# A gated mix of linear attention and an MLP: three of the four row blocks form the MLP's first layer from seven products of half tiles instead of eight

## The chip, the core and the metric

The kernel runs on one core of one Trainium2 chip. The metric is the device time of one execution in microseconds (us), as the median of several runs.

## The reference

```python
x = A_x                                        # 2048 x 512
g = sigmoid((x * gate_w).sum(-1, keepdims=True))
qkv = x @ wqkv                                 # 32 heads of width 16
pq, pk = q @ w_phi, k @ w_phi                  # per head
phi = concat(softmax(p), softmax(-p))          # for pq and for pk
kv, z = phi_k^T v, sum of phi_k                # per head, over all rows
a = (phi_q kv / (phi_q z + 1e-6)) @ wo
b = mish(x @ w1 + b1) @ w2                     # 512 -> 1376 -> 512
out = g * a + (1 - g) * b
```

## The kernel before

**Two passes.** The first pass (`a_ops`, line 289) goes over the 2048 rows in eight chunks of 256: it forms k, v and q, the features of k, the sums `kv` and `z`, and parks q in DRAM (`pqd`). Beside it `w_ops` (line 367) loads the MLP's weights in pieces and splits them. The second pass (`b_ops`, line 512) goes over four blocks of 512 rows, called block 0 to 3 here: it forms phi_q, the attention's output, the MLP and the mix, and stores the result.

**Precision.** Every operand of a large product is a pair of tiles, a rounded high part (`fp32r`) and the rest. A product of two such operands is three matmuls: high by high, high by low, low by high.

**The MLP in a block.** The hidden layer has 11 tiles of 128 units (`ORDER`, line 32); the first one, tile 5, is short and carries the gate's row too. For tile number i of a block: `up` (line 516) is 12 matmuls of 128x128 weights by 128x512 rows of x; `mi` is Mish with the bias on ScalarE (ACT); `hi` rounds to the high part on ACT; `lo` is the low part on GpSimd (POOL); `dn` (`down`, line 559) multiplies by the second layer into four PSUM tiles, 12 matmuls. `df` is `down` of the last tile, `fi` (line 712) mixes and stores one of the four row tiles.

**The attention in a block**, for row tile t: `lq` loads q (SP queue), `mx mn d0 d1` on VectorE (DVE) subtract the extremes, `E` is Exp on ACT, `S T rS D m de rd sc es` on DVE are sums, the denominator and the scaling, `tr` transposes on DVE and stores to DRAM (`ed`); `mv` (line 643) loads two of them back as `eT` with eight DMAs, `nu` multiplies by `kv`, `oh` (ACT) and `ol` (DVE) split the result, `wo` (line 676) is the last product, `ag` (ACT) applies the gate. `gr` takes the gate's row through DRAM and back, `ge gg` make the gate of it. `LX` loads the next block's x, `XH` (ACT) and `XL` (DVE) split it (`x_ops`, line 416).

**What sets the order.** Each engine works through its own queue in the order in which the program issues, and an instruction that waits holds up all behind it; SP's queue of DMA issues is such a queue too. The order is written out by hand in the step tables (lines 37 to 86): `run` (line 201) goes through a table and calls the steps; a step with `+` belongs to the next block, with `'` to the one before. Nothing is moved afterwards (`keep_in_program_order`).

**Buffers.** A tag has a fixed number of buffers which its tiles take in turn, so that a tile waits for the last use of an older one: tag `a` has 3 PSUM tiles (`up`, part of `nu`, every second `wo`), `dn` 4, `kv` 1; `oh` has 2 SBUF tiles (raw weights, the split `nu`), `tx` 2 (raw x, the products `T`), `pq` 3, `eT` 2.

Line 101 of the profile is the helper for every matmul, line 121 that for every ACT instruction.

Of the kernel before, what the change touches and what calls it, by code (L numbers as in the profile page):

```python
# [30 lines left out]
GROW = FA % P  # L31
ORDER = [NFA - 1] + list(range(NFA - 1)) + list(range(NFA, NF))
WARM = 10

# [37 lines left out]
    up0 mi0 hi0 lo0 gr mx2 mn2 d02 d12 mx3 mn3 d03 d13 up1 mi1 hi1 lo1 lq0+ lq1+ E2 E3 hc S2 T2 rS2 D2 m2 de2 rd2 sc2 es2 tr2  # L72
    up2 mi2 hi2 lo2 dn0 S3 T3 rS3 D3 m3 de3 rd3 sc3 es3 tr3 mv1 up3 mi3 hi3 lo3 dn1 up4 mi4 hi4 lo4 dn2
    mx0+ mn0+ d00+ d10+ mx1+ mn1+ d01+ d11+ lq2+ lq3+ up5 mi5 hi5 lo5 dn3 E0+ E1+ ge gg
    S0+ T0+ rS0+ D0+ m0+ de0+ rd0+ sc0+ es0+ tr0+ up6 mi6 hi6 lo6 dn4 up7 mi7 hi7 lo7 dn5 cd nu0 nu1 oh0 ol0 S1+ T1+ rS1+ D1+ LX0 LX1
    m1+ de1+ rd1+ sc1+ es1+ dn6 wo0 ag0 wo1 ag1 oh1 ol1 tr1+ mv0+ dn7 up8 mi8 hi8 lo8 mx2+ mn2+ d02+ d12+ mx3+ mn3+ d03+ d13+
    wo2 ag2 up9 mi9 hi9 lo9 dn8 E2+ E3+ up10 mi10 hi10 lo10 wo3 ag3 XH0+ XL0+ XH1+ XL1+ dn9 df0 fi0 df1 fi1 df2 fi2 df3 fi3
"""
BLOCK = """
    up0 mi0 hi0 lo0 gr lq0+ lq1+ S2 T2 rS2 D2 m2 de2 rd2 sc2 es2 tr2 up1 mi1 hi1 lo1 hc up2 mi2 hi2 lo2 dn0  # L80
    S3 T3 rS3 D3 m3 de3 rd3 sc3 es3 tr3 mv1 up3 mi3 hi3 lo3 dn1 up4 mi4 hi4 lo4 dn2
    mx0+ mn0+ d00+ d10+ mx1+ mn1+ d01+ d11+ lq2+ lq3+ up5 mi5 hi5 lo5 dn3 E0+ E1+ ge gg
    S0+ T0+ rS0+ D0+ m0+ de0+ rd0+ sc0+ up6 mi6 hi6 lo6 dn4 cd nu0 nu1 oh0 ol0 es0+ tr0+ S1+ T1+ rS1+ D1+ LX0 LX1 m1+ de1+ rd1+ sc1+
    es1+ dn5 wo0 ag0 wo1 ag1 oh1 ol1 tr1+ mv0+ dn6 up7 mi7 hi7 lo7 wo2 ag2 mx2+ mn2+ d02+ d12+ mx3+ mn3+ d03+ d13+
    up8 mi8 hi8 lo8 dn7 E2+ E3+ up9 mi9 hi9 lo9 wo3 ag3 up10 mi10 hi10 lo10 dn8 XH0+ XL0+ XH1+ XL1+ dn9 df0 fi0 df1 fi1 df2 fi2 df3 fi3
"""
# [3 lines left out]
def tile_gated_mix(ctx: ExitStack, tc: tile.TileContext, xT, wv, wkT, wqT, bd, w1a, w1b, b1, w2a, w2b, wo, out):  # L90
# [303 lines left out]

# [19 lines left out]
    wob = {}  # L414

    def x_ops(b, load, split):

        raw = {}
        for h in range(2):
            def ld(h=h):  # L420
                raw[h] = k4("xraw", "tx")
                pin(Sy.dma_start(kt(raw[h], SC), xT[2 * b + h]))
# [89 lines left out]
    def b_ops(b):  # L512
        key = ("B", b)
        U, dn, eTs, num, ohl, io, ed = {}, {}, {}, {}, {}, {}, {}

        def up(i):
            f = ORDER[i]
            xh, xl = xb[b]
            ps = psum("up", "a")
            n = 0  # L520
            for w, a in ((0, xh), (1, xh), (0, xl)):
                for k in range(KT):
                    mm(ps, w1_tile(f, w, k), a[:, k, :], start=(n == 0), stop=(n == 3 * KT - 1))
# [35 lines left out]
        def down(i, t):  # L559
            if t not in dn:  # L560
                dn[t] = psum("down", "dn")
            f = ORDER[i]
            h, l = [U[i][x][:, t * P : (t + 1) * P] for x in "hl"]
            for n, (a, w) in enumerate(((h, w2_tile(f, 0)), (h, w2_tile(f, 1)), (l, w2_tile(f, 0))) if i else ((h, w2x["a"]), (l, w2x["b"]))):
                mm(dn[t], a, w, start=(i == 0 and n == 0), stop=(i == (NF - 3 if t == last_t else NF - 1) and n == 2))

# [325 lines left out]
```

## Time and profile before

| | us |
|---|---|
| median of 3 runs (lowest, highest) | 444.73 (444.40, 446.12) |
| span of the profiled execution | 442.5 |
| first pass, to the first `up` | 149.4 |
| block 0, block 1, block 2 (first `up` to first `up`) | 72.5, 72.3, 72.4 |
| block 3 to the end of the span | 76.0 |
| busy in the span: TensorE (PE), DVE, ACT, POOL | 437.8, 313.2, 201.4, 159.6 |

The time of the profiled execution itself is not listed apart from its span; the span runs from its first to its last instruction, and the median of the runs is 2.2 us above it. In the views that follow, "L101 PE MATMUL" names the line of the kernel, the engine and the operation; `out<-in` are tiles by their names in the program. In a list by time, the first column is the start and the second the length, both in us; several equal instructions in a row are merged (`x12`). What stands in brackets at the end of a row is the idle time ahead of it and what ended it. SPq is SP's queue of DMA issues; its rows are the issues, not the transfers.

### The profile page before, as it was taken

The page shows a single profiled execution, that of the slowest core. Times are in us where ns is not written, and L with a number is a line of the kernel's source. Part 1 is how long each engine was busy: PE and PEld are TensorE (multiplying, and loading weights), DVE is VectorE, ACT ScalarE, POOL GpSimd, SP SyncE. Part 2 cuts the span into 40 slices and gives each one's busy share as a digit, 9 for nine tenths or more (in the row PEclk, how much of TensorE's full clock was granted, in tenths as well). Part 3 has the DMA queues.
Part 4 walks back from the last instruction along what each step waited for, and adds up shares of the span by engine and source line. Part 5 has one row for each costly group of instructions (what it writes and reads, how often), then busy time and mean ns, then how long its engine had stood idle before and what let it go on. Part 6 is the DMA issues. An engine that isn't in the chain of part 4 may idle for free.

```text
span 442.5 us, 7179 instructions
## 1 busy us (share of the span) xinstructions
PE 437.8 (99%) x2874; PEld 359.9 (81%) x2874; DVE 313.2 (71%) x420; ACT 201.4 (46%) x286; POOL 159.6 (36%) x100
## 2 busy tenths in 40 slices
PE   8999999999999999999999999999999999999996
PEld 7888888888888888887888878888878888887885
DVE  3987739559699999999999898279679329601103
ACT  3644523533345455736376533646352645341330
POOL 3078694785662453621024120215310222411121
PEclk9999999999999999999999999999999999999999
DMA  7721631524403136425362533222605302310002
GB/s 265 283 96 48 191 120 50 188 86 133 167 29 116 49 84 209 142 101 168 128 205 96 159 124 120 75 96 95 191 0 192 94 2 96 134 57 1 0 0 96
DMA packets 29001, 49.64 MB, mean 112 GB/s; under 512 B 6308, under 2 KB 15012, under 8 KB 28968
## 3 DMA queue, kind: packets, MB, share of 16 engines
q1 hardware_dynamic: 28648, 48.79, 32.9%
q8 instruction: 22, 0.36, 0.3%
q10 hardware_dynamic: 288, 0.39, 0.3%
q14 instruction: 11, 0.09, 0.1%
q0 software_dynamic: 32, 0.01, 0.0%
HBM read 31.73 MB, written 16.79 MB: 110 GB/s over the span
## 4 chain that ended last, share of the span: by engine, by line
PE 98%; DMA 1%; SPq 0%; DVE 0%; issue 0%
PE proj L101 30%; PE up L101 27%; PE down L101 27%; PE wo L101 10%; PE kvp L101 2%; PE num L101 2%; DMA wT<-in_wkT_dram 1%; PE fuse L101 1%; PE rest L101 0%; DVE io L709 0%; SPq L157 0%; SPq L149 0%
## 5 line engine op out<-in xcount | busy, mean ns | idle before, releaser
L543 POOL TENSOR_TENSOR l<-act,h 128x512 fp32r<-128x512 f32 (+1 forms) x44 | 62.6, 1425 | 215.5 <-ACT h L121 192.7
L121 ACT ACTIVATE act<-up,b1s 128x512 f32<-128x512 f32 x44 | 30.3, 688 | 83.1 <-PE up L101 81.0
L330 POOL TENSOR_TENSOR zacc<-zacc,E 128x1024 f32<-128x1024 f32 x16 | 39.7, 2479 | 39.9 <-DVE E L287 31.4
L121 ACT ACTIVATE E<-E 128x1024 f32<-128x1024 f32 x32 | 33.5, 1060 | 36.0 <-DVE E L272 35.9
L287 DVE TENSOR_TENSOR E<-E,Sm 128x1024 f32<-128x1024 f32 x32 | 45.1, 1409 | 1.0
L101 PE MATMUL wo<-woh,ohl 128*128 128x512 f32 x128 | 41.2, 389 | 0.0
L276 DVE TENSOR_REDUCE Sm<-E 128x64 f32<-128x1024 f32 x32 | 38.5, 1204 | 0.0
L101 PE MATMUL down<-w2ah,h 128*128 128x512 f32 x96 | 37.6, 392 | 0.0
L101 PE MATMUL down<-w2al,h 128*128 128x512 f32 x80 | 31.2, 390 | 0.0
L101 PE MATMUL down<-w2ah,l 128*128 128x512 f32 x80 | 31.1, 389 | 0.0
L121 ACT ACTIVATE h<-act 128x512 fp32r<-128x512 f32 (+2 forms) x48 | 30.3, 632 | 1.6
L101 PE MATMUL down<-w2bh,h 128*128 128x512 f32 x78 | 30.6, 392 | 0.0
L101 PE MATMUL down<-w2bl,h 128*128 128x512 f32 x78 | 30.4, 389 | 0.0
L101 PE MATMUL down<-w2bh,l 128*128 128x512 f32 x78 | 30.4, 389 | 0.0
L431 DVE TENSOR_TENSOR xbl<-xraw,xbh 128x1024 fp32r<-128x1024 f32 x8 | 10.9, 1378 | 27.1 <-ACT xbh L121 27.1
L256 DVE TENSOR_REDUCE mx<-proj 128x32 f32<-128x512 f32 x16 | 11.0, 689 | 25.5 <-PE proj L101 25.5
L101 PEld LDWEIGHTS wo<-woh,ohl 128*128 128x128 f32 x128 | 24.0, 188 | 5.0
L121 ACT ACTIVATE io<-wo,g_sb 128x512 f32<-128x512 f32 x16 | 11.0, 690 | 36.0 <-PE wo L101 34.7
L121 ACT ACT_TABLE_LOAD x19 | 24.4, 1283 | 3.5 <-PE up L101 3.2
L101 PE MATMUL up<-xbh,w1ah 128*128 128x512 f32 x96 | 25.8, 390 | 0.0
L101 PE MATMUL up<-xbh,w1al 128*128 128x512 f32 x96 | 25.7, 389 | 0.0
L101 PE MATMUL up<-xbl,w1ah 128*128 128x512 f32 x96 | 25.7, 389 | 0.0
(125 smaller groups left out, 978.3 us busy)
## 6 DMA issues: line engine op xcount, KB each, us to landing
ed<-E SPq DMA_DIRECT2D x16, 512.0 KB, 2.9
eT<-ed SPq DMA_DIRECT2D x64, 128.0 KB, 3.2
xraw<-in_xT_dram SPq DMA_DIRECT2D x15, 512.0 KB, 4.3
pqd<-qs SPq DMA_DIRECT2D x16, 256.0 KB, 2.1
pq<-pqd SPq DMA_DIRECT2D x16, 256.0 KB, 3.8
out_dram<-io SPq DMA_DIRECT2D x15, 256.0 KB, 2.0
raw<-in_w1a_dram SPq DMA_DIRECT2D x3, 512.0 KB, 4.6
raw<-in_w2a_dram SPq DMA_DIRECT2D x3, 512.0 KB, 3.7
```

Of the source, the lines that this page charges most:

```text
L101: return pin(nc.tensor.matmul(*a, **k))
L121: return pin(A_.activation(out_, in_, fn, **k))
L256: pin(V.tensor_reduce(d[name], hv(src()), axis=AX.X, op=op))
L276: pin(V.tensor_reduce(d["S"], hv(d["E"][:, :]), axis=AX.X, op=ALU.add))
L287: pin(eng.tensor_mul(hv(d["E"][:, :]), hv(d["E"][:, :]), d["S"][:, :, None].to_broadcast([P, 2 * H, DH])))
L330: at(key, f"z{t}", lambda d=d: pin(G_.tensor_add(zacc, zacc, d["E"])))
L431: pin(V.tensor_sub(xb[b][1][:, :, sl], kt(raw[h], SC), f32(xb[b][0][:, :, sl])))
L543: pin(G_.tensor_sub(U[i]["l"][:n, :], U[i]["a"][:n, :], f32(U[i]["h"][:n, :])))
```

## The change

It touches blocks 1 to 3 and, to prepare them, the first pass and block 0.

- **Products.** In blocks 1 to 3 the ten full hidden tiles are taken as five pairs g (tile g and tile 6+g, `PAIRS`). For a pair, with the weight's halves A11 to A22 (two k tiles of one hidden tile each) and the halves B11 to B22 of x (two k tiles by 256 rows), the four half results come from seven products by Strassen's scheme (Winograd's form): A11 by B11, A12 by B21, S1 by T1, S2 by T2, S3 by T3, S4 by B22, A22 by T4. S are sums of weights, T sums of x. Each product is six matmuls 256 wide, so 42 for a pair; `up` had 24 matmuls 512 wide for two tiles.
- **Steps of a pair.** On PE `s1` (18 matmuls), `s2` (12), `s3` (6), `s4` (6); they add up in one PSUM tile, so that its state is copied or added in between: `c1`, `c2` are ACT copies, `a1 a2 a3` DVE additions, 128x256 each. `M0 M1` is Mish (M1 in two halves), `H0 H1` and `L0 L1` take the place of `hi` and `lo`.
- **Sums of weights.** S1 to S4 are made in DRAM in the first pass: four DRAM to DRAM copies on SP in chunk 1 (`sc`), seven accumulating DMAs on POOL in chunks 2 to 4 (`sa`). For each pair, in block 0 (g 0 and 1) or block 1 (g 2 to 4), `ls` loads the four sums (4 DMAs), `hs` (ACT) and `os` (POOL) split them, `ts` stores them to DRAM (2 DMAs); `tp` stores the split A11, A12, A22 there (4 DMAs, all in block 0). `load_units` (`wl`, 7 DMAs of 256 KB a pair; `wi`, 10 at the end of block 0) brings them back, one pair or two ahead, into 12 buffers of tag `wS`.
- **Sums of x.** `TT` (DVE), `TH` (ACT), `TL` (POOL) make T1 to T4 with their parts for each of blocks 1 to 3; `XL` of block 1 goes from DVE to POOL.
- **Order.** New tables for blocks 0 to 3. `df fi` of row tiles 2 and 3 go into the next block, `nu1` in blocks 1 to 3 goes behind the pairs.

In the program the matmuls go from 2354 to 2624, SP's instructions from 202 to 366, DVE's from 422 to 477, ACT's from 290 to 372, POOL's from 105 to 136; ACT's table loads stay at 20. The core of the diff:

```diff
+PAIRS = [NFA - 1] + [f for g in range(NFB) for f in (g, NFA + g)]
+UNITS = "S1", "S2", "S4", "S3", "A11", "A12", "A22"
 MID = """
...
-    S1 rS1 ml1 z1 ve1 q0 qe0 st0 q1 qe1 st1
+    S1 rS1 ml1 z1 ve1 sc sa q0 qe0 st0 q1 qe1 st1
 BLOCK0 = """
...
-    up4 mi4 hi4 lo4 WH1 WL0 dn2 E2 S2 T2 rS2 D2 m2 de2 rd2 sc2 es2 tr2 up5 mi5 hi5 lo5 WL1 dn3 E3 ge gg up6 mi6 hi6 lo6 dn4
-    up7 mi7 hi7 lo7 dn5 S3 T3 rS3 D3 m3 de3 rd3 sc3 es3 tr3 mv1 up8 mi8 hi8 lo8 dn6
-    mx0+ mn0+ d00+ d10+ mx1+ mn1+ d01+ d11+ lq2+ lq3+ up9 mi9 hi9 lo9 dn7 E0+ E1+ S0+ T0+ LX0 rS0+ D0+ m0+ de0+ rd0+ sc0+
-    up10 mi10 hi10 lo10 dn8 dn9 cd nu0 nu1 oh0 ol0 es0+ tr0+ XH0+ XL0+ S1+ T1+ rS1+ LX1 df0 df1 wo0 ag0 wo1 oh1 ol1 ag1 D1+ fi0
-    m1+ de1+ rd1+ sc1+ df2 df3 wo2 ag2 fi1 XH1+ XL1+ es1+ fi2 wo3 ag3 fi3 tr1+ mv0+
+    up4 mi4 hi4 lo4 WH1 WL0 dn2 E2 S2 T2 rS2 D2 m2 de2 rd2 sc2 es2 tr2 up5 mi5 hi5 lo5 WL1 tp0 dn3 E3 ge gg up6 mi6 hi6 lo6 ls0 dn4
+    up7 mi7 hi7 lo7 hs0 os0 dn5 S3 T3 rS3 D3 m3 de3 rd3 sc3 es3 tr3 mv1 tp1 ts0 up8 mi8 hi8 lo8 dn6
+    mx0+ mn0+ d00+ d10+ mx1+ mn1+ d01+ d11+ lq2+ lq3+ ls1 up9 mi9 hi9 lo9 hs1 os1 tp2 dn7 E0+ E1+ S0+ T0+ LX0 rS0+ D0+ LX1 tp3 tp4 ts1 m0+ de0+ rd0+ sc0+
+    up10 mi10 hi10 lo10 wi dn8 XH0+ XH1+ dn9 cd nu0 nu1 oh0 XL0+ XL1+ ol0 TT0+ TT1+ TT2+ TT3+ TH0+ TL0+ TH1+ TL1+ es0+ tr0+ S1+ T1+ rS1+ df0 df1 wo0 ag0
+    TH2+ TL2+ wo1 ag1 oh1 ol1 TH3+ TL3+ D1+ fi0 m1+ de1+ rd1+ sc1+ wo2 ag2 fi1 es1+ wo3 ag3 tr1+ mv0+
+END = """
+    s3_4 a3_4 wo0 ag0 s4_4 M1_4 H1_4 L1_4 mx3+ mn3+ d03+ d13+ dn9 XH0+ XH1+ XL0+ XL1+ TT0+ TT1+ TT2+ TT3+ wo1 ag1 TH0+ TL0+ nu1 oh1 ol1 TH1+ TL1+
+    E2+ E3+ df0 df1 wo2 ag2 TH2+ TL2+ wo3 ag3 TH3+ TL3+ fi0 fi1
 BLOCK1 = """
+    up0 mi0 gr ls2 mx2 mn2 hi0 lo0 s1_0 c1_0 a1_0 d02 d12 df2' fi2' df3' fi3' hs2 os2 mx3 mn3 s2_0 c2_0 a2_0 M0_0 H0_0 L0_0 ts2 hc dn0 wl_0 d03 d13 E2 E3 ge
+    s3_0 a3_0 S2 s1_1 c1_1 s4_0 M1_0 a1_1 H1_0 L1_0 T2 rS2 D2 ls3 dn1 s2_1 c2_1 a2_1 M0_1 H0_1 L0_1 hs3 os3 gg m2 de2 rd2 sc2 es2 tr2 ts3 wl_1 dn2
+    s3_1 a3_1 S3 s1_2 c1_2 s4_1 M1_1 a1_2 H1_1 L1_1 T3 rS3 D3 ls4 dn3 s2_2 c2_2 a2_2 M0_2 H0_2 L0_2 hs4 os4 m3 de3 rd3 sc3 es3 tr3 mv1 ts4 wl_2 lq0+ lq1+ dn4
+    s3_2 a3_2 s1_3 c1_3 s4_2 M1_2 a1_3 H1_2 L1_2 mx0+ mn0+ d00+ d10+ dn5 s2_3 c2_3 a2_3 M0_3 H0_3 L0_3 wl_3 mx1+ mn1+ d01+ d11+ lq2+ lq3+ E0+ E1+ dn6
+    s3_3 a3_3 s1_4 c1_4 s4_3 M1_3 a1_4 H1_3 L1_3 mx2+ mn2+ d02+ d12+ dn7 s2_4 c2_4 a2_4 cd nu0 M0_4 oh0 H0_4 L0_4 ol0 wl_4 LX0 LX1 dn8
 """ + END
+BLOCK = """
+    up0 mi0 gr S0 T0 hi0 lo0 s1_0 c1_0 a1_0 rS0 D0 m0 de0 rd0 sc0 df2' fi2' df3' fi3' s2_0 c2_0 a2_0 M0_0 H0_0 L0_0 hc es0 tr0 wl_0 dn0 S1
+    s3_0 a3_0 T1 s1_1 c1_1 s4_0 M1_0 a1_1 H1_0 L1_0 rS1 D1 m1 de1 rd1 sc1 dn1 s2_1 c2_1 a2_1 M0_1 H0_1 L0_1 es1 tr1 mv0 wl_1 lq0+ lq1+ dn2
+    s3_1 a3_1 S2 s1_2 c1_2 s4_1 M1_1 a1_2 H1_1 L1_1 T2 rS2 D2 dn3 s2_2 c2_2 a2_2 M0_2 H0_2 L0_2 m2 de2 rd2 sc2 es2 tr2 wl_2 dn4
+    s3_2 a3_2 mx0+ mn0+ s1_3 c1_3 s4_2 M1_2 a1_3 H1_2 L1_2 d00+ d10+ mx1+ mn1+ d01+ d11+ lq2+ lq3+ dn5 s2_3 c2_3 a2_3 M0_3 H0_3 L0_3 ge E0+ E1+ gg S3 wl_3 dn6
+    s3_3 a3_3 T3 s1_4 c1_4 s4_3 M1_3 a1_4 H1_3 L1_3 rS3 D3 m3 de3 rd3 sc3 es3 dn7 s2_4 c2_4 a2_4 tr3 mv1 cd nu0 M0_4 oh0 H0_4 L0_4 ol0 wl_4 LX0 LX1
 """
+BLOCK2 = BLOCK + "mx2+ mn2+ d02+ d12+ dn8" + END
+BLOCK3 = BLOCK + """
+    dn8 s3_4 a3_4 wo0 ag0 s4_4 M1_4 H1_4 L1_4 wo1 ag1 nu1 oh1 ol1 df0 fi0 wo2 ag2 df1 fi1 wo3 ag3 mo df2 fi2 df3 fi3
 """
...
+            def ls(g=g, d=d):
+                d["l"] = k4("sr", "oh", F32R)
+                for i, x in enumerate(UNITS[:4]):
+                    pin(Sy.dma_start(f32(d["l"][:, i * SC : (i + 1) * SC]).rearrange("p (k e) -> p k e", k=2), sums[x][:, :, g, :]))
+            def hs(d=d):
+                d["h"] = k4("sh", "oh", F32R)
+                act(d["h"], f32(d["l"][:, :]))
+            def os(d=d):
+                pin(G_.tensor_sub(d["l"], f32(d["l"][:, :]), f32(d["h"][:, :])))
...
+    def load_units(todo):
+        for g, x in todo:
+            if 0 <= g < NFB * (NB - 1):
+                units[g, x] = unit("w" + x, "wS")
+                pin(Sy.dma_start(f32(units[g, x][:, :]), prod[g % NFB][:, UNITS.index(x), :]))
...
+            def add(ps, u, x, start=False):
+                w, (xh, xl) = units[G, u], operand(x)
+                n = 0
+                for o, a in ((0, xh), (SC, xh), (0, xl)):
+                    for k in range(2):
+                        mm(ps, w[:, o + k * P : o + (k + 1) * P], a[:, k, :], start=(start and n == 0), stop=(n == 5), skip_group_check=True)
+                        n += 1
+            def s1():
+                d["b"] = psum("upb", "a")
+                add(d["b"][:, lo_], "S1", "T1", True)
+                add(d["b"][:, hi_], "A12", "B21")
+                d["a"] = psum("upa", "a")[:, lo_]
+                add(d["a"], "A11", "B11", True)
+            def c1():
+                d["A"] = [k2("act", "hl") for _ in range(2)]
+                act(d["A"][1][:, hi_], d["b"][:, lo_])
+                act(d["A"][0][:, lo_], d["a"])
+            def s2():
+                add(d["a"], "S2", "T2")
+                add(d["b"][:, lo_], "S4", "B22")
+            def s3():
+                add(d["a"], "S3", "T3")
+            def s4():
+                add(d["a"], "A22", "T4")
+            def c2():
+                act(d["A"][0][:, hi_], d["a"])
+            def sum_(j, cs, ps):
+                o = d["A"][j][:, cs]
+                pin(V.tensor_add(o, ps, o))
...
+            at(key, f"wl_{g}", lambda: load_units([(G + 1, "S2"), (G + 1, "S4"), (G + 1, "S3"), (G + 2, "S1"), (G + 2, "A12"), (G + 2, "A11"), (G + 1, "A22")]))
+            at(key, "wi", lambda: load_units([(0, x) for x in ("S1", "A12", "A11", "S2", "S4", "S3")] + [(1, x) for x in ("S1", "A12", "A11")] + [(0, "A22")]))
```

More of the change, by code (lines that the diff above doesn't have):

```diff
@@ L70 @@
+    TH2+ TL2+ wo1 ag1 oh1 ol1 TH3+ TL3+ D1+ fi0 m1+ de1+ rd1+ sc1+ wo2 ag2 fi1 es1+ wo3 ag3 tr1+ mv0+
+"""
+END = """
+    s3_4 a3_4 wo0 ag0 s4_4 M1_4 H1_4 L1_4 mx3+ mn3+ d03+ d13+ dn9 XH0+ XH1+ XL0+ XL1+ TT0+ TT1+ TT2+ TT3+ wo1 ag1 TH0+ TL0+ nu1 oh1 ol1 TH1+ TL1+
+    E2+ E3+ df0 df1 wo2 ag2 TH2+ TL2+ wo3 ag3 TH3+ TL3+ fi0 fi1
 """
 BLOCK1 = """
-    up0 mi0 hi0 lo0 gr mx2 mn2 d02 d12 mx3 mn3 d03 d13 up1 mi1 hi1 lo1 lq0+ lq1+ E2 E3 hc S2 T2 rS2 D2 m2 de2 rd2 sc2 es2 tr2
-    up2 mi2 hi2 lo2 dn0 S3 T3 rS3 D3 m3 de3 rd3 sc3 es3 tr3 mv1 up3 mi3 hi3 lo3 dn1 up4 mi4 hi4 lo4 dn2
@@ L74 @@
[L74 to L77, printed above, removed]
-"""
[L79 to L85, printed above, removed]
+    up0 mi0 gr ls2 mx2 mn2 hi0 lo0 s1_0 c1_0 a1_0 d02 d12 df2' fi2' df3' fi3' hs2 os2 mx3 mn3 s2_0 c2_0 a2_0 M0_0 H0_0 L0_0 ts2 hc dn0 wl_0 d03 d13 E2 E3 ge
@@ L384, in wl @@
                 h, l = W[n_][0]
-                pin(G_.tensor_sub(l[:, cs], raws[n_, cs.start], f32(h[:, cs])))
+                pin(G_.tensor_sub(l[:, o : o + n], r, f32(h[:, o : o + n])))
             at(("A", c), f"ldw{j}", ld)
@@ L414, in tile_gated_mix @@
     wob = {}
+    xt = {}
     def x_ops(b, load, split):
```

181 lines of the change are left out of this document (150 added, 31 removed).

## The prediction

> **What bounds the kernel now.** I read the page's head, then the chain of waits, then the busy times by stretch (here block 0 and block 1, from first `up` to first `up`).
>
> ```profile
> span 442.5 us, 7179 instructions
> PE 437.8 (99%) x2874; PEld 359.9 (81%) x2874; DVE 313.2 (71%) x420; ACT 201.4 (46%) x286; POOL 159.6 (36%) x100
> ...
> PE 98%; DMA 1%; SPq 0%; DVE 0%; issue 0%
> ```
>
> ```profile
> core 0: us, PE busy (x) PEld busy (x) DVE busy (x) ACT busy (x) POOL busy (x), PEclk, DMA share, GB/s
> 149.35:221.82 72.47, 72.47 (x378) 59.14 (x377) 69.35 (x93) 38.42 (x53) 21.98 (x15) 1.00 0.41 131
> 221.82:294.10 72.28, 72.28 (x377) 59.07 (x376) 57.08 (x80) 38.96 (x53) 15.04 (x11) 1.00 0.36 117
> ```
>
> PE is the bound without a gap: its matmuls make 98% of the chain, and in a block of 72.3 to 72.5 us it is busy all the time. So whatever shortens PE's stream counts in full, and whatever makes PE wait counts in full too. The column of DVE says what to fear: in block 0 it is busy for 69.35 of 72.47 us, so nothing that it does late is caught up there.
>
> **1. PE's own work.** The chain gives the pace of a 512-wide matmul, the list by time that of the 256-wide ones at the kernel's end (12 starts, each with its own weights).
>
> ```profile
> 181.31 2.72 PE up L101 x12
> ```
>
> ```profile
> 437.58 0.28 PE L101 MATMUL rest<-w2bh,h 128*128 128x256 f32 x1
> ...
> 438.90 0.28 PE L101 MATMUL rest<-w2bh,l 128*128 128x256 f32 x1
> ```
>
> 2.72/12 = 0.2267 us for 512; (438.90 - 437.58)/11 = 0.120 us for 256, more than half. A pair took 24 x 0.2267 = 5.44 us and takes 42 x 0.120 = 5.04 us: 0.40 us less, and with 15 pairs **6.0 us less**. The other bound for 0.120 is the length of one weight load, 0.188 us, if loads didn't overlap in a long stream:
>
> ```profile
> L101 PEld LDWEIGHTS up<-xbh,w1ah 128*128 128x128 f32 x96 | 17.9, 188 | 3.8
> ...
> L101 PEld LDWEIGHTS rest<-w2bh,h 128*128 128x128 f32 x4 | 0.8, 191 | 0.0
> ```
>
> Then 630 matmuls would cost 630 x 0.068 = 43 us more. But the last row's loads of 0.191 us do run at 0.120 us, so I take 0.120. The Trainium skill (TensorE: Matmul & The Clock Gate, "Back-to-back issue gap") has N/2.4 + 2.5 ns for a matmul alone: 109 and 216 ns, which would save 0.59 us a pair, 8.9 us in all. The rows have 120 and 227 ns; the measurement decides.
>
> **2. First pass.** The four copies and seven accumulations are not in the trace. Their first reader is `ls0`, some 100 us later, so only the issuing counts: on POOL at least the 0.68 us of its one DMA; a sum has two runs in each partition, where that DMA has one, so at most (an estimate from that row) 1.4 us each, 5.4 us for the four in chunk 2.
>
> ```profile
> 1.78 0.68 POOL L186 DMA_DIRECT2D b1s<-in_b_dram  x1
> ...
> 73.89 2.39 POOL L330 TENSOR_TENSOR zacc<-zacc,E 128x1024 f32<-128x1024 f32 x1 [6.42 <-DVE E L287]
> ```
>
> POOL is idle for 6.4 us right behind, and its next split of x is wanted a chunk later. I take 0; if that cover failed, 2 us.
>
> **3. Block 0.** Its matmuls stay, but loads are put into SP's queue and `hs` into ACT's. The rows are SP's queue, PE, ACT and DVE in block 0, then the landings of DMAs (last number, us) and lengths (mean ns).
>
> ```profile
> 186.79 9.39 SPq L628 DMA_DIRECT2D ed<-E  x2
> 196.28 4.32 SPq L649 DMA_DIRECT2D eT<-ed  x8
> 200.64 0.91 SPq L607 DMA_DIRECT2D pq<-pqd  x2
> 201.59 0.43 SPq L422 DMA_DIRECT2D xraw<-in_xT_dram  x1
> ```
>
> ```profile
> 206.16 1.96 PE L101 MATMUL num<-eT,kvb 64*32 64x256 f32 x64
> ...
> 221.82 1.07 PE L101 MATMUL up<-xbh,w1ah 128*128 128x512 f32 x4
> ```
>
> ```profile
> 195.73 0.63 ACT L121 ACTIVATE h<-act 128x512 fp32r<-128x512 f32 x1
> 196.38 1.28 ACT L121 ACT_TABLE_LOAD   x1
> 198.96 1.06 ACT L121 ACTIVATE E<-E 128x1024 f32<-128x1024 f32 x1 [1.30 <-DVE E L272]
> ...
> 203.73 0.69 ACT L121 ACTIVATE act<-up,b1s 128x512 f32<-128x512 f32 x1
> ```
>
> ```profile
> 193.33 1.23 DVE L287 TENSOR_TENSOR E<-E,Sm 128x1024 f32<-128x1024 f32 x1
> ...
> 195.76 0.64 DVE L256 TENSOR_REDUCE mx<-pq 128x32 f32<-128x512 f32 x1
> ...
> 201.24 1.21 DVE L276 TENSOR_REDUCE Sm<-E 128x64 f32<-128x1024 f32 x1
> ...
> 205.16 0.23 DVE L634 TENSOR_TENSOR Dn<-Dn,Sm 128x64 f32<-128x64 f32 x1
> ```
>
> ```profile
> ed<-E SPq DMA_DIRECT2D x16, 512.0 KB, 2.9
> ...
> xraw<-in_xT_dram SPq DMA_DIRECT2D x15, 512.0 KB, 4.3
> ...
> out_dram<-io SPq DMA_DIRECT2D x15, 256.0 KB, 2.0
> ...
> raw<-in_wo_dram SPq DMA_DIRECT2D x8, 128.0 KB, 2.8
> ...
> raw<-in_w1b_dram SPq DMA_DIRECT2D x1, 256.0 KB, 2.9
> ```
>
> ```profile
> L121 ACT ACTIVATE xbh<-xraw 128x1024 fp32r<-128x1024 f32 x8 | 8.2, 1050 | 0.1
> ...
> L669 DVE TENSOR_TENSOR ohl<-num,ohl 128x512 fp32r<-128x512 f32 x16 | 10.2, 678 | 17.9 <-ACT ohl L121 17.9
> ...
> L121 ACT ACTIVATE ohl<-num 128x512 fp32r<-128x512 f32 x16 | 8.8, 596 | 9.6 <-PE num L101 8.2 <-PE wo L101 1.4
> ```
>
> An issue costs SP 0.43 us (0.54 for `eT`), and a small load lands 2.8 us after it. SP reaches 200.6 with `mv1` as now, since that waits for DVE's transpose. New behind it: `tp1` and the first `ts0`, 5 issues, to 202.8; its store lands at 205.7 (2.9). `ls1` needs that store's buffer, so its four loads go out from 205.7, the last at 207.0, and land at **209.8**. ACT reached this place at 196.4; there `hs1` now waits for 209.8 and holds up all behind it: `hs1` 1.05, table 1.28, two E, table 1.28, `mi10` 0.69 put the end of `mi10` at 216.1 (204.4 now). PE needs `mi10` for the second PSUM tile of `nu1` (three of tag `a`), which it reaches half way through `num`, at 207.1: **9.0 us of idle PE**. What is late next: E0+ ends at 213.1, DVE's S, T, rS, D (205.16 - 201.24 = 3.9) at 217.0; LX1 waits for D0+ (tag `tx`), and behind it SP issues `tp3 tp4` (8) and `ts1` (2), at 220.9 and 221.4, landed at 224.3. `oh0` takes the buffers of pair 1's sums and waits for that; `oh0` 2 x 0.6, `ol0` let `wo0` start at 225.1. `wo0 wo1` (24 x 0.2267 = 5.4) end at 230.5, `ag1` and `oh1` (1.3) let `wo2` start at 231.8; it waits for the second `ol1`, behind TT, es0, tr0, S1, T1, rS1 on DVE, at 234.7; `wo3` ends at 237.8. Now it is 221.8, and 1.4 us of `df` have left the block: **17.4 us lost**. With issues at 0.38 (`ge_sb` below) and landings at 2.0 it is 14, with 0.54 and 4.3 it is 20 or more. (`hs0` waits in the same way, for `ls0` behind the store at 186.8 and `tp0`, until about 193.5 where ACT is there at 185.5; `mi8` then comes at 195.3, and PE wants it at 200.2, so that costs nothing.)
>
> **4. Blocks 1 to 3.** Without waits a block takes 72.3 - 2.0 = 70.3 us. PE now waits for ACT (`c1`, `c2`), DVE (`a3` ahead of `s4`) and unit loads. I took the queues step by step from the block's start, with the rows above and these: es and tr 2.43, eight of mx to d1 5.48, S to D 3.92 (differences of DVE's starts above), and a 256-wide copy and addition:
>
> ```profile
> L121 ACT ACTIVATE wkh<-fuse 128x256 fp32r<-128x256 f32 x7 | 2.3, 387 | 6.1 <-PE fuse L101 6.1
> ...
> L750 DVE TENSOR_TENSOR wkl<-fuse,wkh 128x256 fp32r<-128x256 f32 x8 | 2.8, 416 | 1.3 <-ACT wkh L121 1.3
> ```
>
> ```profile
> 226.25 4.27 SPq L649 DMA_DIRECT2D eT<-ed  x8
> 230.62 0.23 SPq L585 DMA_DIRECT2D gd<-gr  x1
> 232.70 0.38 SPq L586 DMA_DIRECT2D ge_sb<-gd  x1
> ```
>
> *Block 1, 16 us* (times from its start at 237.8). (a) DVE ends tr1+ at 3.1: after `ol1` it has D, two `fi`, m to sc, es and tr, 6.2 us. On SP the store of it (0.4), `mv0+` (4.3), and `gr`'s way through DRAM and back (230.62 to 232.70, and 0.4) stand ahead of `ls2`, whose loads go out from 10.4 to 11.7 and land at 14.5. `hs2` (1.05) stands ahead of `c2_0` (0.39) on ACT: 15.9. PE is at `s3_0` after up0, s1, df, s2, dn0 = 2.72 + 2.16 + 1.36 + 1.44 + 1.81 = 9.5: 6.4 lost. (b) On ACT `hc`, a table load, E2, E3 stand ahead of `c1_1`, which ends at 23 though `s1_1` ended at 19; then M1_0 with another table load, and L0_0 and L1_0 on POOL, hold `dn1` and `dn2`: 3.5. (c) S2 of pair 3 is loaded behind tr3, `mv1` and `ts4`: tr3 ends at 41, the issue is at 46, it lands at 49; PE is there at 45.5: 4. (d) `lq0+` goes out behind that load, mx0+ on DVE waits for it, and `a2_3`, `a3_3` behind: 2.5.
> *Block 2, 10 us.* (a) Behind S0, T0 DVE stops until `c1_0`, then has rS0 to sc0 (2.8) and two `fi` (1.5) ahead of `a2_0`; `dn0` waits for `fi3'`, `s4_0` for `a3_0` behind es0, tr0, S1: 4. (b) S2 of pair 2 goes out behind tr1 (ends at 24) and `mv0` at 29 and lands at 32; PE is there at 30: 2.4. (c) tr3 ends at 57; `mv1` (8 issues) and `wl_4` (7) put LX at 65, landed at 70. XH on ACT, then XL, four TT and `ol1` on DVE follow, and `wo2`, which PE reaches at 71, waits: 3.8.
> *Block 3, 6 us:* (a) and (b) of block 2.
> Each wait is an issue time plus a landing behind a step of DVE, less PE's own time to that place. At 0.38 and 2.0 the three blocks cost 22, at 0.54 and 4.3 about 40; I take 32, by the middle rows (0.43; 2.8 to 2.9). The transfers as such have room: 105 units of 256 KB are 27 MB in 215 us, and the DMA share now is 0.36 of block 1.
>
> **Sum.** Span 442.5 - 6.0 + 17.4 + 32 = 485.9; the median of the runs lies 2.2 above the span (444.7 and 442.5): **488 us**.
>
> **Rivals.**
> *Hidden (the other side, faster):* the waits don't cost PE anything and only the 6.0 us are left: 438.7. It decides in block 0: `ls1`'s sums must be in before ACT is there at 196.4. Against it: `mv1` alone keeps SP until 200.6 in the trace. For it: ACT is idle for 33 of block 1's 72 us, so there is room for the work, if not in this order.
> *Only the block edges:* the waits inside the pairs vanish (PE is already late there, so the loads are in); block 0's 17.4, 6 of `hs2` and 3.8 of LX remain: 444.7 - 6.0 + 27 = 466.
> *PE slow after idling:* PE is idle for 5 to 9 us ahead of `nu1`, `wo0` and block 1's `s3_0`; if the next step of 12 matmuls then ran at half pace, it would cost 2.7 us more each time: 488 + 8 = 496. For or against it this trace has nothing: PE never idles that long between matmuls. The Trainium skill (same page, "What's actually happening") says that the clock is halved after an idle window of some 3.4 us until PE has been busy for as long; no row here shows it.
> *Weight loads as the pace* (0.188 us): 43 - 6 us more instead of 6 less, which hide part of the waits in blocks 1 to 3: 444.7 + 37 + 30 = 512. The rows of `rest` speak against it, but they are only 12 in a row.
>
> **How the numbers follow.** Forecast 0.56, only the edges 0.20, slow after idling 0.13, hidden 0.06, weight loads 0.03, others 0.02. Own range of the forecast: 17.4 and 32 at their low ends (14 and 22) give 475, at their high ends (20 and 40) 499. The range reaches from the edges' case with a cheaper block 0 (466 - 5 = 461) to 503 for the slow clock with dear issues. A measurement of this kernel can tell about 0.5% from no change. Faster by more than that only if hidden: 0.06; within 0.5% 0.01; slower 0.93.
>
> **What would show it.** `rest`-like pace of 0.120 us in the pairs; the end of `hs1` near 211 and idle PE of 9 us in `nu`, then of 5 us ahead of `wo0`; SP's queue with `eT` issues ahead of the unit loads that PE waits for; the second pass 43 us longer, the first unchanged. I am wrong if ACT isn't held up by `hs1`, or if PE's idle time in blocks 1 to 3 is under 20 us.

## The result, and the profile after

The changed kernel takes **523.4 us** (median of 4 runs, 521.3 to 525.6), the kernel before 444.6 us beside it: a ratio of **1.177** (95% interval 1.173 to 1.181). 488 us was forecast, with a range of 461 to 503. The sign was right, the size was not: 78.8 us were lost, where 43.4 were forecast.

First the head of the page and its chain of waits:

```profile
span 523.9 us, 8288 instructions
PE 459.2 (88%) x3144; PEld 380.0 (73%) x3144; DVE 348.2 (66%) x475; ACT 231.5 (44%) x368; POOL 203.4 (39%) x131
...
PEclk9999999999999999659978977998979997999999
...
PE 24%; DVE 23%; DMA 14%; SPq 4%; ACT 4%; issue 3%; POOL 1%; DVEq 0%; ACTq 0%; POOLq 0%
```

PE's matmuls made 98% of the span before and make 24% of it now, no more than DVE; DMA landings and SP's issues have another 18%. (The chain can be followed back only to 138 us, so the first pass is not in these shares.) So the second pass no longer has the length of PE's stream, but that of a chain that runs through all the engines. The busy times by block show the same (the pass before, then blocks 0 to 3):

```profile
0.00:149.59 149.59, 147.81 (x1364) 122.99 (x1365) 113.89 (x145) 65.55 (x98) 97.63 (x65) 1.00 0.61 182
149.59:248.82 99.23, 76.94 (x377) 59.90 (x371) 78.22 (x95) 42.51 (x59) 40.23 (x23) 0.88 0.60 191
248.82:350.24 101.42, 81.72 (x468) 68.46 (x467) 57.83 (x81) 47.10 (x77) 27.42 (x17) 0.88 0.63 208
350.24:441.34 91.10, 78.64 (x468) 66.03 (x467) 56.87 (x89) 42.10 (x72) 22.05 (x16) 0.91 0.54 182
441.34:523.90 82.56, 74.06 (x479) 62.63 (x477) 41.35 (x68) 34.23 (x63) 16.09 (x12) 1.00 0.44 150
```

The first pass is unchanged (149.59 us for 149.35). The blocks take 99.2, 101.4, 91.1 and 82.6 us, where they took 72.5, 72.3, 72.4 and 76.0. No other engine is full either: DVE is busy for 78 of block 0's 99 us and for 58 of block 1's 101. PE's waits by what ended them (us in total, times, the longest):

```profile
PE upa L109 <- DMA wS<-prod: 13.6, 4, 6.0
PE num L109 <- ACT act L129: 10.2, 1, 10.2
PE wo L109 <- DVE ohl L879: 8.5, 2, 7.4
PE upa L109 <- ACT act L129: 8.4, 4, 5.6
PE wo L109 <- ACT ohl L129: 8.2, 2, 6.9
PE upa L109 <- DVE act L739: 6.5, 5, 2.2
```

Nearly every wait of the forecast is there, with its place and its releaser: `nu1` 10.2 us (9.0 forecast), `wo0` 7.4, `s3_0` of block 1 5.6, the unit loads 13.6, `wo2` of block 2 6.9. Only the 3.5 us of `dn1` and `dn2` in block 1 for POOL are nearly missing (0.5 here). The waits add up to 59 us with the small ones, where about 49 were forecast. PE's busy time is above that of before as well, by 21.5 us in the four blocks (311.4 for 289.8), where 6.0 less was forecast. So two questions were open: whether the slow clock (PEclk 0.88 to 0.91) is the cause, and which part of the change the time belongs to.

### The profile page after: what moved, and what is told of

It is laid out like the page before. It is cut to its first block, busy times and chain, and to the rows that moved or that the text cites. A ratio compares the mean times of both kernels' runs of the same rounds, so it can differ in the third digit from the quotient of the medians.

```text
span 523.9 us, 8288 instructions
## 1 busy us (share of the span) xinstructions
PE 459.2 (88%) x3144; PEld 380.0 (73%) x3144; DVE 348.2 (66%) x475; ACT 231.5 (44%) x368; POOL 203.4 (39%) x131
## 4 chain that ended last, share of the span: by engine, by line
PE 24%; DVE 23%; DMA 14%; SPq 4%; ACT 4%; issue 3%; POOL 1%; DVEq 0%; ACTq 0%; POOLq 0%
PE down L109 9%; PE wo L109 6%; PE upa L109 5%; DVE E L295 4%; DMA wS<-prod 3%; DVE E L836 3%; DMA ed<-E 3%; PE upb L109 3%; DVE Sm L284 2%; DMA xraw<-in_xT_dram 2%; DVE Dn L825 2%; DMA prod<-sr 2%; SPq L859 2%; DMA sr<-sumS 1%; DVE T L821 1%
## 5 line engine op out<-in xcount | busy, mean ns | idle before, releaser
L758 POOL TENSOR_TENSOR l<-act,h 128x512 fp32r<-128x512 f32 x30 | 41.6, 1386 | 149.0 <-ACT h L129 143.1
L109 PE MATMUL wo<-woh,ohl 128*128 128x512 f32 x128 | 44.7, 415 | 16.7 <-DVE ohl L879 8.5
L739 DVE TENSOR_TENSOR act<-upb,act 128x256 f32<-128x256 f32 x30 | 12.6, 421 | 58.1 <-ACT act L129 34.4
L295 DVE TENSOR_TENSOR E<-E,Sm 128x1024 f32<-128x1024 f32 x32 | 49.3, 1542 | 0.9
L109 PE MATMUL upa<-xth,wS 128*128 128x256 f32 x120 | 21.2, 302 | 22.0 <-DMA wS<-prod 13.6
L109 PEld LDWEIGHTS upa<-xth,wS 128*128 128x128 f32 x120 | 18.9, 202 | 27.1 <-issue 15.2
L668 POOL TENSOR_TENSOR l<-act,h 128x512 fp32r<-128x512 f32 (+1 forms) x14 | 19.8, 1420 | 38.4 <-ACT h L129 16.4
L554 POOL TENSOR_TENSOR xtl<-xt,xth 128x512 fp32r<-128x512 f32 x12 | 21.0, 1762 | 30.3 <-ACT xth L129 30.2
L129 ACT ACTIVATE act<-act,b1s 128x512 f32<-128x512 f32 (+1 forms) x30 | 18.4, 615 | 28.7 <-DVE act L739 28.6
L129 ACT ACTIVATE act<-upa 128x256 f32<-128x256 f32 x30 | 11.4, 382 | 43.5 <-PE upa L109 43.5
L256 POOL TENSOR_TENSOR xl<-xraw,xh 128x512 fp32r<-128x512 f32 x14 | 21.1, 1705 | 18.2 <-ACT xh L129 18.2
```

The costliest lines, as they stand in the source:

```text
L109: return pin(nc.tensor.matmul(*a, **k))
L129: return pin(A_.activation(out_, in_, fn, **k))
L256: pin(eng.tensor_sub(xs[c][1][j], kt(rawx[c], SC)[:, 2 * j : 2 * j + 2, :], f32(xs[c][0][j])))
L295: pin(eng.tensor_mul(hv(d["E"][:, :]), hv(d["E"][:, :]), d["S"][:, :, None].to_broadcast([P, 2 * H, DH])))
L554: pin(G_.tensor_sub(l, sub(j), f32(h[:, :])))
L668: pin(G_.tensor_sub(U[i]["l"][:n, :], U[i]["a"][:n, :], f32(U[i]["h"][:n, :])))
```

## The experiments

**The clock.** Is it the half clock behind PE's long waits that the forecast missed? This run keeps PE busy in the five longest ones.

```diff
+FILL = {(0, "f0"): 38, (0, "f1"): 28, (1, "f0"): 20, (1, "f1"): 22, (2, "f1"): 26}
-... dn9 cd nu0 nu1 oh0
+... dn9 cd nu0 f0 nu1 oh0          (f1 ahead of wo0, s2_3, wo2; f0 ahead of s3_0)
+        mm(dn[3][:32, :], zz, w2_tile(0, 0), start=False, ...)     # zz is zero
```

> The changed kernel with 134 matmuls of a zero tile put into PE's five longest waits (38 ahead of nu1 and 28 ahead of wo0 in block 0, 20 ahead of s3_0 and 22 ahead of s2_3 in block 1, 26 ahead of wo2 in block 2): they add nothing to the sums and fill 134 x 0.2267 = 30.4 of the 36 us that PE waits there. Theory (the clock halves after a long wait): the waits stay, but what follows each runs at the full clock at once, 1.2 to 2.9 us less each, 6 to 14 us in all: 509 to 517 us. Rival (PE's busy time of the four blocks is 21.5 us above that of the kernel before, in place of 6 below, because 256-wide matmuls are slower among other work, whatever the waits): 521 to 526 us.

Measured: 522.2 us, ratio 1.177 (1.172 to 1.181): the same as without. The profile says why that is a result. PE's list of waits in this run, and the granted clock by block:

```profile
PE upa L110 <- DMA wS<-prod: 8.5, 3, 3.3
...
PE num L110 <- ACT act L130: 3.3, 1, 3.3
```

```profile
150.38:253.27 102.89, 92.57 (x444) 67.52 (x438) 78.60 (x97) 42.53 (x59) 39.47 (x23) 0.95 0.59 187
253.27:352.09 98.82, 87.29 (x509) 69.35 (x508) 53.92 (x79) 47.15 (x77) 27.25 (x17) 0.95 0.66 211
352.09:441.78 89.69, 82.24 (x494) 66.48 (x492) 56.69 (x89) 42.01 (x72) 21.66 (x16) 0.96 0.56 185
```

Over half of the lost clock came back (0.95, 0.95, 0.96 for 0.88, 0.88, 0.91), and without its filler PE was busy for some 7 us less in the four blocks (336.3 less 31.8 of filler, for 311.4). Yet the time did not fall: in this profile blocks 1 and 2 are 2.6 and 1.4 us shorter, and block 0 is 3.7 us longer. PE's waits and the filler together are 66 us, where the waits were 59: what PE saved it waited. So the theory in the expectation fell, and these 7 us were worth nothing. They are a quarter of the 27 us by which PE was busier than forecast (21.5 and 6.0), though; what the rest is worth, this run doesn't show, since behind the waits of 3.3 and 3.4 us that are left in block 0 the matmuls start 0.43 us apart again.

**The parts, taken away one after the other.** First the whole preparation of the units goes, then their reloading.

```diff
- ... sc sa ... tp0 ls0 hs0 os0 ts0 ...     (and those of pairs 1 to 4)
-  pin(Sy.dma_start(f32(units[g, x][:, :]), prod[g % NFB][:, UNITS.index(x), :]))
+  pin(Sy.dma_start(f32(units[g, x][:, :]), pqd[(g % NFB) * P : (g % NFB + 1) * P, :]))
...
-  if 0 <= g < NFB * (NB - 1):                # second run only, with the lines above
+  if g == 0:
...
-  w, (xh, xl) = units[G, u], operand(x)
+  w, (xh, xl) = units[0, u], operand(x)
```

> The changed kernel without the preparation: the copies and accumulations of the first pass, ls, hs, os, ts and tp are left out, and the unit loads, as many and as large, read another tensor (so the MLP's first layer has wrong weights). Theory (block 0 is late through ACT behind hs1 and oh0 behind ts1, block 1 through hs2, and the clock halves behind these waits): block 0 falls from 99 to 75 to 80 us, block 1 from 101 to 83 to 88: 480 to 490 us. Rival (it is the traffic: landings of 4.4 to 4.8 us where 2.9 was expected, and the 27 MB of unit loads are the larger part of it): 505 to 515 us.

> As without the preparation, and every pair takes the seven units of the first one, loaded once (so the MLP's first layer is wrong): no unit is reloaded. What is left of the change is the seven products, the additions and the new order. Theory (the reloads behind mv on SP's queue make the rest of the waits in the blocks, 13.6 us by the waits, and slow stretches behind them): 20 to 25 us below the run without the preparation, 455 to 470 us. Rival (256-wide matmuls and the additions are themselves the cost): no more than 8 us below it, and above 472.

Measured: 488.6 us without the preparation (95% interval of the ratio 1.098 to 1.104), and 469.6 us with resident units (1.054 to 1.059). So the preparation costs **34.8 us**, the reloads **19.0 us**, and what is then left of the change, without any DMA of its own, still costs **25.0 us**. By the forecast's own terms these three were 24, 15 and 5. In the first of the two runs block 0 fell to 78.5 us and block 1 to 84.9 us, as the theory had it. In the second PE's own pace is seen undisturbed: the six matmuls of a step take 0.71 to 0.72 us, 0.12 each.

```profile
334.28 0.64 PE L109 MATMUL upa<-xth,wS 128*128 128x256 f32 x4
334.75 0.40 PE L109 MATMUL upa<-xtl,wS 128*128 128x256 f32 x2
334.99 0.64 PE L109 MATMUL upb<-xth,wS 128*128 128x256 f32 x4
...
335.71 0.64 PE L109 MATMUL upb<-xbh,wA 128*128 128x256 f32 x4
```

So by their pace the seven products save the 6.0 us of the forecast, and 25.0 + 6.0 = 31 us of waits and what follows them stand against that, with every unit in place. DVE's list by time has them:

```profile
L739 DVE TENSOR_TENSOR act<-upb,act 128x256 f32<-128x256 f32 x30 | 12.6, 421 | 40.5 <-ACT act L129 29.1 <-PE upb L109 11.4
...
L739 DVE TENSOR_TENSOR act<-upa,act 128x256 f32<-128x256 f32 x15 | 6.1, 410 | 4.4 <-PE upa L109 4.4
```

The 45 additions are 18.7 us of work, and DVE stands idle for another 44.9 us ahead of them, until ACT has copied or PE has multiplied. PE's own list shows only 3.3 us of waits for additions in this run. Four runs on top of this one tell what is behind it.

**Additions and the sums of x.** All four keep the units resident.

```diff
 def operand(x):                          # without the sums of x
-    return [... for a in xt[b, int(x[1]) - 1]]
+    return operand({"T1": "B11", "T2": "B12", "T3": "B21", "T4": "B22"}[x])
 ...
-at(key, f"a1_{g}", lambda: sum_(...))    # without additions: a1, a2, a3
 ...
-    o = d["A"][j][:, cs]                 # additions on a scratch tile
-    pin(V.tensor_add(o, ps, o))
+    o = units["s"]
+    pin(V.tensor_add(o, o, o))
```

> As the run with resident units, and without the sums of x: TT, TH and TL are left out and the products take quarters of x in their place (the first layer is wrong). Theory (at the end of a block LX, XH, XL and four TT on DVE stand ahead of ol1, and PE waits for ol1): 6 to 12 us below the run with resident units, 457 to 464 us, most of it in block 0, of 79.7 us there. Rival (the additions of the products are what PE waits for): 466 us or more.

> As the run with resident units, and without the 45 additions of products on DVE (a1, a2, a3 are left out, the copies c1 and c2 stay; the first layer is wrong). Theory (the additions stand in DVE's queue behind other work, and PE waits 3.3 us for them directly): 3 to 8 us below the run with resident units, 462 to 467 us. Rival (they are the larger half of the 25 us that this run stands above the kernel before): 450 to 458 us.

> As the run with resident units, without the sums of x and without the additions of products (the first layer is wrong): what is left is PE's stream of seven products, the copies on ACT and the new order. Theory (the 25 us are DVE's added work in series with PE): 444 to 453 us, not far above PE's own 438.7. Rival (the new order of the blocks itself, or the table loads of Mish and copies on ACT): 456 us or more.

> As the run with resident units, but each of the 45 additions is done on a scratch tile of the same 128x256 size that nobody waits for and that waits for nobody (the products are not added, so the first layer is wrong): DVE has the same number of operations, without the waits. Theory (without the additions that run fell by 16.7 us because an addition makes DVE's queue wait for PE and ACT, 40.5 us of idle DVE ahead of them, and everything behind it on DVE with it): 452 to 457 us, as without additions. Rival (it is the 45 x 0.42 = 19 us of work on DVE): 463 to 470 us.

Measured: without the sums of x 465.4 us (4.2 less, somewhat short of what was expected); without additions **452.8 us (16.7 less)**, where I had expected 3 to 8, so the rival was right; without both 449.9 us; and with the additions on a scratch tile **453.9 us**. In this last run the list by time shows more work for DVE than the real additions are, but no idle time ahead of it:

```profile
L742 DVE TENSOR_TENSOR scr<-scr 128x256 f32<-128x256 f32 x45 | 26.0, 577 | 0.1
```

26 us of work on DVE cost 1 us; 18.7 us of work that waits and is waited for cost 16.7. The blocks say where: blocks 1 to 3 take 80.0, 77.9 and 79.4 us with resident units and 72.7, 74.3 and 76.6 with the additions on a scratch tile; block 0, which has no additions, takes 80.2 and 78.9. So it is not the work, but the coupling: an addition holds up what stands behind it on DVE until PE and ACT are there, and then PE's next step, or Mish on ACT, waits for an addition that stands behind something else. One round of this, from the chain of the run with resident units:

```profile
271.69 4.19 DMA pq<-pqd
275.88 0.67 DVE mn L264
...
277.06 0.69 DVE E L280
277.75 0.33 DVE act L739
278.08 0.59 DVE mx L264
278.68 0.60 DVE mn L264
...
279.79 0.69 DVE E L280
280.47 0.34 DVE act L739
...
280.86 0.98 PE upa L109 x6
```

PE's `s4` needs an addition of 0.34 us; that stands behind eight operations on the next block's rows and one more addition, and those behind a load that landed at 275.9.

**The preparation.** Which of it costs the 34.8 us?

```diff
- ... ls1 ... hs1 os1 ... ts1 ... ls2 ... hs2 os2 ... ts2   (first run)
- ... sc sa ... ls hs os ts of all pairs, tp stays          (second)
- ... os0 ... os1 ... os2 ... os3 ... os4                   (third)
```

> The changed kernel without the sums of pairs 1 and 2 (their ls, hs, os and ts are left out; the loads of these eight units read another tensor, so the first layer is wrong for two pairs). Stores of A11, A12, A22 and the sums of pairs 0, 3 and 4 stay. Theory (the forecast's steps 3 and 4a: of the preparation only hs1 with ts1 in block 0 and hs2 in block 1 stand on the path): nearly all of the 34.8 us that leaving out the whole preparation saved, 26 to 33 us less: 490 to 498 us. Rival (every part of the preparation costs its share of SP's and ACT's queues): two of five pairs, about 14 us less: 505 to 513 us.

> The changed kernel without any sums of w1 (copies and accumulations of the first pass, ls, hs, os, ts are left out, and the loads of these units read another tensor, so the first layer is wrong); the stores tp of A11, A12, A22 stay, 20 issues of SP in block 0. Theory (the stores wait for nothing and cost only their issues): 488 to 494 us, as without the preparation. Rival (they are the rest that leaving out two pairs' sums didn't explain, through SP's time and the slower landings): 497 to 508 us.

> The changed kernel without the five os on POOL (the sums' low parts are stored as the whole sums, so the first layer is wrong): 5 x 2.7 us less on POOL. Theory (while POOL subtracts, two-operand work on DVE beside it is stretched, E at 2.9 us in place of 0.68 and at 2.4 in place of 1.24, and os is on the way from ls to ts): 6 to 12 us less, 511 to 518 us. Rival (os is hidden): 521 to 526 us.

Measured: without the sums of pairs 1 and 2 511.6 us (11.8 less); with the stores `tp` alone 494.6 us (6.0 above no preparation at all); without `os` 524.8 us, no gain. So the first and the third theory fell, and the second missed its range by 0.6 us. `hs1`, `ts1` and `hs2`, on which the forecast put 23.8 us, are worth 11.8; the stores, which it counted as issues, cost 6.0; the other 17 us are left for the sums of pairs 0, 3 and 4, by subtraction (no run takes these away alone). By the blocks of the profiles: block 0 takes 99.2 us, 89.4 without pair 1's sums, 86.2 with the stores alone and 78.5 without any preparation. Block 1 takes 101.4 us, 95.2 without pair 2's sums, and 85.0 without any. So pairs 3 and 4 cost block 1 some 10 us. Its chain in the changed kernel shows one way:

```profile
302.17 4.86 DMA prod<-sr
...
307.12 0.32 SPq L485
...
308.44 0.42 SPq L485
308.91 6.08 DMA pq<-pqd
...
315.62 0.68 DVE mn L264
...
320.21 0.34 DVE act L739
...
320.60 1.65 PE upa L109 x6
```

SP stores pair 4's sums and, after three loads for pair 3, loads pair 4's first unit from the same tensor. So it stands still for the store's landing (4.86 us), issues four loads (1.8), then `lq0+`, which lands after 6.08; then come DVE's `mx` to `d1`, the addition of pair 3, PE.

**The order.** If it is a chain of queue places, moving the places must help, with all the work left in. Four runs of the whole change, each on top of the one before:

```diff
-BLOCK1 ... es3 tr3 mv1 ts4 wl_2 lq0+ lq1+        # 1: S2, S4, S3 of the next pair (wa), LX
+BLOCK1 ... wa_2 m3 de3 rd3 sc3 es3 tr3 mv1 ts4 wl_2 lq0+ lq1+
-BLOCK  ... es1 tr1 mv0 wl_1 lq0+ lq1+ ... tr3 mv1 ... wl_4 LX0 LX1
+BLOCK  ... wa_1 wl_1 lq0+ lq1+ es1 tr1 mv0 ... LX0 LX1 wa_4 wl_4 tr3 mv1
-BLOCK0 ... WL1 tp0 ... tr3 mv1 tp1 ts0 ... hs1 os1 tp2 dn7 E0+ ... LX1 tp3 tp4 ts1 ... mi10 hi10    # 2
+BLOCK0 ... ldo1 tp0 tp1 ... lq1+ tp2 tp3 tp4 ... WL1 ls0 ... tr3 ts0 mv1 ... E0+ ... LX1 ... mi10 hi10 hs1 os1 lo10 ts1
-BLOCK1 ... mv1 ts4 wl_2 lq0+ lq1+                # 3
+BLOCK1 ... mv1 lq0+ lq1+ ts4 wl_2
-BLOCK0 ... ag3 tr1+ mv0+ BLOCK1 up0 mi0 gr ls2   # 4
+BLOCK0 ... ag3 ls2+ tr1+ mv0+ BLOCK1 up0 mi0 gr
```

> The changed kernel with another order on SP's queue in blocks 1 to 3: the loads of S2, S4 and S3 of the next pair, and those of the next block's x, go out ahead of tr, mv and ts instead of behind them. Theory (the forecast's steps 4: these loads are late because they stand behind DVE's transposes on SP): the 13.6 us that PE waits for units go nearly, and the 6.9 us ahead of wo2 in block 2, with the slow stretches behind them: 18 to 28 us less, 495 to 505 us. Rival (the loads are late because the DMA queues are full, and the order doesn't matter): 516 to 526 us.

> The whole change with the new order of SP's queue in blocks 1 to 3 of the earlier run (508.6 us), and block 0 ordered anew: the stores tp go out at the block's begin, WL1 and ls0 ahead of tr2, ts0 ahead of mv1, hs1 and os1 behind mi10 and E0+, LX0 and LX1 ahead of ts1. Theory (block 0's 99 us are a chain of landings and queue places, of which the earlier LX and E0+ take out some 8 to 12 us, while oh0 still waits for ts1): 494 to 502 us. Rival (DVE is full in block 0, and its work sets the end whatever SP does): 505 to 510 us.

> The whole change with the reordered queues (497.2 us before this step), and in block 1 lq0+ and lq1+ ahead of ts4 and the unit loads behind it. Theory (SP waits 4 to 6 us for the landing of ts4 ahead of the loads of pair 4's units, and lq0+, then mx0+ to d10+ and the additions of pair 3 on DVE, then PE, are late by that and by the four loads of 1.7 us): 5 to 8 us less, 489 to 492 us. Rival (DVE and PE are held by the loads of the units themselves): 495 to 499 us.

> As the run with lq0+ and lq1+ moved, and ls2 goes out at the end of block 0 ahead of tr1+, mv0+ and gr's two issues instead of behind them. Theory (ls2 lands some 8 us earlier, so ACT isn't held by hs2 at c2_0, and PE not at a2_0 and s3_0): 4 to 8 us below that run. Rival (ACT's other work there, hc, two table loads, E2 and E3, sets dn1 whenever hs2 is done): no more than 2 us below it.

Measured: 508.6, 497.2, 491.7 and **487.1 us** (the last 1.089 to 1.097 of the kernel before): 36 us came back by order alone. The first step ended 3.6 us above its range, the others within theirs. In the first, blocks 2 and 3 took 78.7 and 79.5 us, as with resident units (77.9 and 79.4): there, reloading costs next to nothing if the loads don't stand behind DVE's stores. Steps 3 and 4 together take block 1 from 98.2 to 88.9 us, and with it the way through `lq0+` and that through `ls2` are shown. The last run is the best that this study found of the whole change; it is still 42.6 us above the kernel before.

## Why the prediction was wrong

**The steps that held.** The pace of PE's own work (0.120 us for 256 wide) and the first pass at nothing are as forecast; weight loads as the pace and the hidden case are out. The 6.0 us themselves don't show in PE's busy time even in the three runs with the fewest waits, those without additions or with free ones: it is 289.9 to 290.2 us in the four blocks, for 289.8 before. Block 0, with the matmuls of before, is already busy for 1.3 to 2.0 us more there. The mechanism of step 3 is in the trace: `hs1` began at 214.3 (209.8 forecast), held ACT for 13.1 us, `nu1` waited 10.2 us, `oh0` and `wo0` came after `ts1`. The steps of the other blocks are among PE's waits at their places, but for that of `dn1` and `dn2`.

**The step that failed is step 4's sum, "I took the queues step by step".** It walked PE through its waits and added them, as if each engine that PE waits for worked on in the meantime. What it left out, but for the wait for `c1_0` in block 2 (a), is that the additions make DVE wait too. By groups, taken away one after the other as above:

| group, with the forecast's terms | forecast | measured |
|---|---|---|
| preparation: step 3's 17.4, block 1 (a) 6.4 | 23.8 | 34.8 |
| reloads behind DVE's stores: block 1 (c), (d), block 2 (b), (c), block 3 (b) | 15.1 | 19.0 |
| products, additions, x's sums, new order: block 1 (b), block 2 (a), block 3 (a) = 11.1, less 6.0 | 5.1 | 25.0 |
| sum | 44.0 | 78.8 |

(The 6 us of block 3 are split here as 3.6 and 2.4; the parts add up to 0.6 more than the forecast's rounded blocks.) **20 us of the 35 are the third line**, and most of it is the additions: 16.7 us by the run without them, 15.7 by that with free ones. (The groups are told apart by taking them away in this order; another order might split them otherwise.) The forecast had only the direct waits of PE for them, a few us in each block.

**11 us are the preparation.** Here too a mechanism was seen and the rest left out. Step 3 put all 17.4 us of block 0 on pair 1's sums; without them block 0 is only 9.8 us shorter, since the stores ahead of LX, `xraw`'s landing and four TT on DVE ahead of `ol1` then end nearly as late. And for the sums of pairs 3 and 4 there was no term beyond `ts4`'s place ahead of the unit loads: they cost block 1 some 10 us. The store that SP waits for ahead of the next load of the same tensor is part of it: 5.5 us came back when `lq0+` and `lq1+` went ahead of it (497.2 to 491.7). The landings were mis-sized as well: 2.8 to 2.9 us were taken for a load of 256 KB, and the units took 4.4 to 4.8; the loads of x, 512 KB each, took 6.5 where they took 4.3 before:

```profile
wS<-prod SPq DMA_DIRECT2D x60, 256.0 KB, 4.4
wA<-prod SPq DMA_DIRECT2D x45, 256.0 KB, 4.8
...
xraw<-in_xT_dram SPq DMA_DIRECT2D x15, 512.0 KB, 6.5
```

**The rival of the slow clock** (13%, 496 us) was right in its mechanism and wrong in its price. Behind the wait of 7.4 us ahead of `wo0` the changed kernel's matmuls start 0.427 us apart, and at 0.23 only from 236.5 on:

```profile
232.93 0.79 PE L109 MATMUL wo<-woh,ohl 128*128 128x512 f32 x1 [7.37 <-DVE ohl L879]
233.52 0.63 PE L109 MATMUL wo<-wol,ohl 128*128 128x512 f32 x1
233.95 0.63 PE L109 MATMUL wo<-woh,ohl 128*128 128x512 f32 x1
...
236.51 1.35 PE L109 MATMUL wo<-woh,ohl 128*128 128x512 f32 x5
```

The Trainium skill's halved clock after idling (TensorE: Matmul & The Clock Gate, "What's actually happening") agrees with these rows. But with over half of the lost clock given back the time stayed the same within the intervals. The rest of the lost clock was not tried, so it is shown for the part given back alone that PE's pace did not count on a path through other engines.

**What stays open.** Blocks 2 and 3 differ by up to 5 us between profiles of runs that have the same work there (88.0 to 91.1 and 81.9 to 86.7 us); that was not followed up, and the blocks' spans above are to be read with it. Of the 449.9 us without additions and sums of x, some 11 us stand above PE's own stream; the profile of that run has over half of them in block 0 (79.1 us), where LX1, XH1 and `oh0` have new places; no run separates these.

## What to carry to other kernels

When a change puts a second engine into PE's loop (multiply, add on DVE, go on), it is not the added work that must be priced but the coupling: list what stands ahead of each addition in its engine's queue, and what stands behind it while it waits. Here 26 us of uncoupled work cost 1 us and 18.7 us of coupled work cost 16.7. And adding up PE's waits is a forecast only as long as PE is the bound; once no engine is busy throughout, the path must be walked through all of them, and moving places in the queues, loads ahead of waiting stores above all (25 of the 36 us that came back here, with all the work left in), is worth trying before work is taken out.

## What was not expected of the hardware

DVE's work with two operands in SBUF stood still while POOL subtracted: in block 0 of the changed kernel an operation that takes 0.60 to 0.68 us otherwise took 2.88, until just after POOL's end.

```profile
198.71 0.68 DVE L278 TENSOR_TENSOR E<-pq,mx 128x512 f32<-128x512 f32 x1
198.78 2.86 POOL L460 TENSOR_TENSOR sr<-sr,sh 128x1024 fp32r<-128x1024 f32 x1 [11.43 <-ACT sh L129]
199.31 2.88 DVE L280 TENSOR_TENSOR E<-mn,pq 128x512 f32<-128x512 f32 x1
```

The Trainium skill (SBUF — State Buffer, "SBUF: two separate sides") has the two engines share a pair of ports, which one holds for a whole instruction; these rows agree. For the time it was nothing: without the five `os` nothing was gained (POOL's other subtractions stayed).

The clock fell after shorter waits than the rival of the slow clock had it, but not by the length of the wait alone. In the run with filler, five starts behind a wait of 2.35 us took 2.09 us, 0.42 each:

```profile
247.87 2.29 PE L110 MATMUL wo<-woh,ohl 128*128 128x512 f32 x5 [2.35 <-DVE ohl L889]
249.96 0.63 PE L110 MATMUL wo<-wol,ohl 128*128 128x512 f32 x1
```

In the changed kernel four 256-wide starts took 0.82 us behind a wait of 2.19 us, about 0.21 each, but only 0.55 us, near the whole pace, behind one of 2.82 us. What decides between them is not shown here.

```profile
284.08 1.02 PE L109 MATMUL upa<-xth,wA 128*128 128x256 f32 x4 [2.19 <-DVE act L739]
284.90 0.63 PE L109 MATMUL upa<-xtl,wA 128*128 128x256 f32 x2
...
473.87 0.71 PE L109 MATMUL upa<-xth,wS 128*128 128x256 f32 x4 [2.82 <-DMA wS<-prod]
474.42 0.40 PE L109 MATMUL upa<-xtl,wS 128*128 128x256 f32 x2
```
